# Block 1's first product: three of four pairs by seven products, with operand sums made by adding transfers and on VectorE

## The chip, the cores and the metric

The kernel runs on one core of a Trainium2 chip. The metric is the device time of one execution in microseconds (us); the time of the kernel before is the median of three runs. The engines are TensorE (PE in the profile; its weight loads are PEld), VectorE (DVE), ScalarE (ACT), GpSimd (POOL) and SyncE (SP). SyncE, ScalarE and GpSimd also issue DMA transfers.

## The reference

Inputs: q, k, v of shape (4, 8, 768, 64) (batch, heads, time, head dimension), `w_in` (512, 2048) and `w_out` (2048, 512). First a recurrent attention, then a feed-forward layer with a sigmoid gelu:

```python
for t in range(S):
    state = gamma[None, :, None, None] * state + einsum('bhd,bhe->bhde', k[:, :, t], v[:, :, t])
    y[:, :, t] = scale * einsum('bhd,bhde->bhe', q[:, :, t], state)
x = y.transpose(0, 2, 1, 3).reshape(B * S, H * D)       # 3072 x 512
h = x @ w_in                                            # first product, 3072 x 2048
g = h * (1.0 / (1.0 + exp(-1.702 * h)))
out = g @ w_out                                         # second product, 3072 x 512
```

Everything is float32. The two weights are given as 64-bit floats and are narrowed to float32 in the kernel.

## The kernel before, in words

**Blocks.** The time axis is cut into chunks of 64 steps; one chunk of two batches is 128 tokens, and 24 chunks make 6 blocks of 4 chunks (512 tokens). For each block the attention writes x (for block 1 into `X1`, a view of `W2[:, 6]`), the first product makes the hidden values G, and the second product makes the output. Chunks 0 to 7 (blocks 0 and 1) are attended in an opening part, interleaved with the narrowing of the weights; later chunks are attended between the units of the products.

**Forms of a product.** Blocks 0 and 1 do the first product plainly: `up0` in halves of 256 tokens, `up1` (lines 420 to 428) with all 512 tokens for one of 16 column tiles f of 128 hidden columns. A float32 matmul is two TensorE instructions, so one call of `up1` is 4 matmuls, 8 instructions with 512 moving columns. From block 2 on, `up(d)` (lines 465 to 507) does the first product in the form with seven products in place of eight: a pair d of `w1` pairs (512 hidden columns, 512 tokens) is cut into 2 x 2 quarters, seven products of quarter sums are taken, and the four results are put together by additions. Its operand sums are made ahead on GpSimd (`sums_x`, `sums_w1`). One of its products is 4 matmuls, 8 instructions with 256 moving columns. The second product of blocks 0 and 1 is `down`, also with seven products of 4 units each; later blocks use `down49`.

**Weights.** `W1A` holds the first weight's pairs p = 0 to 3, `W1B` p = 4 to 7; each pair has seven slots of 256 columns, of which slots 0 to 3 are the quarters and slots 4 to 6 hold hidden values of block 0 while that block lasts. The narrowing of one weight tile has the steps `fetch` (a transfer on SyncE, L180), `start` (ScalarE, L207, named `abs` in the written order), `half` (three VectorE instructions, L211 to L213) and `rest` (three, L217 to L222). Three raw buffers take turns, so tile i + 3 is fetched once the `rest` of tile i is done. Tiles 0 to 7 are the first weight, 8 to 15 the second.

**Order.** The opening part is a list of names, written out by hand (lines 845 to 862); each name calls a step of `works`. Steps that go through `pin` keep this order on their engine. TensorE's order is all as written. What isn't pinned (the W2 sums of `sums_w2`, lines 445 to 449, the aging of the state, the loads of later chunks' keys and values) is placed on its engine by the planner of the language. In the opening part `up1.f` is a column tile of block 1's first product and `gate1.f` its gelu on ScalarE (`hidden`, L393), which reads PSUM and writes G. Accumulators in PSUM have two tags, x and y, of two buffers each.

**After the opening part.** The loop over blocks from line 866 on starts with block 0's second product: the units of `P_` in `down`, four (d = 0 to 3) for each of seven products n. Next to unit numbers stand other steps: the W2 sums after units 1, 3, 5 and 7, chunk 8's transposition after unit 2 and its scores after unit 5, chunk 9's transposition after unit 14. `late_loads` (lines 788 to 790) issues the loads of chunks 8 and 9 on SyncE.

Of the kernel before, what the change touches and what calls it, by code (L numbers as in the profile page):

```python
# [13 lines left out]
P = 128  # L14
# [14 lines left out]
def kernel(  # L29
# [38 lines left out]
    CB = 4  # L68
# [43 lines left out]
    def w1(p):  # L112

        return (W1A, p) if p < NP // 2 else (W1B[p // 2 - 2], p % 2)
# [3 lines left out]
    def pin(i):  # L118
        return tc.keep_in_program_order(i) if ordered[0] else i
# [308 lines left out]
        return G[:, p, ab:4:2, :], h  # L428


    def sums_w1(p):
        t, q1 = w1(p)
        w = [t[:, q1:q1 + 2, s] for s in range(7)]
        pool.tensor_add(w[4], w[2], w[3])
        pool.tensor_sub(w[6], w[0], w[2])
        pool.tensor_sub(w[5], w[4], w[0])
        pool.tensor_sub(w[2], w[1], w[5])
# [16 lines left out]
    def sums_g(m, p):  # L454
        a = [g(m, p, s) for s in range(4)]
        tc.keep_in_program_order(dve.tensor_add(a[3], a[2], a[3]))
        tc.keep_in_program_order(dve.tensor_sub(a[2], a[0], a[2]))
        tc.keep_in_program_order(dve.tensor_sub(a[0], a[3], a[0]))

    def sums_g_late(m, p):  # L460
        a = [g(m, p, s) for s in range(2)]
        tc.keep_in_program_order(pool.tensor_sub(a[1], a[1], a[0]))
# [209 lines left out]
    def down(m):  # L672

        acc, kept = {}, {}
        b, t0 = m * CB // NC * 2, m * CB % NC * D
        rows = out.rearrange("(b t) (e c) -> e t b c", b=B, c=EH)[:, t0:t0 + TH, b:b + 2, :] \
            .rearrange("e (h p) b c -> h e p b c", p=P)

        def keep(name, tag, src):
            kept[name] = one.tile([P, 2, EH], F32, name=name, tag=tag)  # L680
            act.activation(kept[name], src, AF.Copy)

        def put(th, e, a, b):
            o = two.tile([P, 2, EH], F32, name="o")
            dve.tensor_add(o, a, b)
            tc.keep_in_program_order((pool if m < NB - 1 else act).dma_start(rows[th, e], o))

        def last_part(d, halves={}):

            n = d // (NP // 4)  # L690
            if d % (NP // 4) == 0:
                halves[n] = ps.tile([P, EH], F32, name="pd", tag="xy"[n])
            for p in range(NP // 2 * (d % 2), NP // 2 * (d % 2 + 1)):
                pe.matmul(halves[n], g1(m, p, 1)[:, n * P:(n + 1) * P], W2[:, 3, p, :], start=(p == 0), stop=(p == NP - 1))
            if d % 2:
                o = two.tile([P, 2, EH], F32, name="o")
                dve.tensor_add(o[:, 0], halves[n], kept["t"][:, n])
                act.dma_start(rows[0, 1][:, n], o[:, 0])

        def part(key, sa, sb, new, last, d, then):  # L700
            if m == NB - 1 and key == "x2":
                last_part(d)
                return
            if d == 0 and new:
                acc[key] = ps.tile([P, 2, EH], F32, name="pd", tag=key[0])
            p0 = acc[key]
            for p in range(2 * d, 2 * d + 2):
                for n in range(2):
                    pe.matmul(p0[:, n, :], g1(m, p, sa)[:, n * P:(n + 1) * P], W2[:, sb, p, :],  # L709
                              start=(new and p == 0 and n == 0), stop=(last and p == NP - 1), skip_group_check=True)  # L710
            if d == NP // 2 - 1:
                then(p0)

        def then_p5(y):
            kept["t"] = one.tile([P, 2, EH], F32, name="t", tag="s1")
            dve.tensor_add(kept["t"], y, kept["u"])

        def then_p7(x):
            keep("vv", "s3", x)
            put(1, 0, acc["y1"], kept["vv"])  # L720
            put(1, 1, acc["y2"], kept["vv"])

        P_ = [("x", 0, 0, True, False, lambda x: keep("p1", "s1", x)),
              ("y0", 1, 2, True, True, lambda y: put(0, 0, y, kept["p1"])),
              ("y1", 3, 1, True, True, lambda y: None),
              ("x", 0, 5, False, False, lambda x: keep("u", "s2", x)),
              ("y2", 3, 4, True, True, then_p5),
              ("x", 2, 6, False, True, then_p7),
              ("x2", 1, 3, True, True, lambda y: put(0, 1, y, kept["t"]))]
        todo = []  # L730
        for n, (key, sa, sb, new, last, then) in enumerate(P_):
            for d in range(NP // 2):
                def unit(key=key, sa=sa, sb=sb, new=new, last=last, d=d, then=then, n=n):
                    part(key, sa, sb, new, last, d, then)
                    if n == 2:
                        sums_g(m, 2 * d)
                    if n == 4 and d == 3:
                        for p in range(0, NP, 2):
                            sums_g_late(m, p)
                todo.append(unit)  # L740
        return todo


# [42 lines left out]
                                        ap=[[0, D], [1, HP]])))  # L786

    def late_loads():
        load(2 * CB, "qkv")
        load(2 * CB + 1, "qk")  # L790

    def halves_anew():

# [15 lines left out]
        "causal": causal, "rows": rows,  # L809
        "rowd": lay_rowd, "whole": lay_whole, "late_loads": late_loads, "anew": halves_anew,  # L810
        "warm": keep_warm}
    for j in range(2 * CB):
        for name in "qkv":
            works[f"{name}{j}"] = lambda j=j, name=name: load(j, name)
        works |= {f"{name}{j}": lambda j=j, do=do: do(j) for name, do in (
            ("turn", turn), ("turned", turned), ("decay", decay), ("masked", masked), ("state", by_state),
            ("x", output), ("aged", aged), ("updated", updated))}
        for f in (None, *range(2 * CB)):
            works[f"step{j}" + ("" if f is None else f"-{f}")] = lambda j=j, f=f: attend(j, f)
        works[f"step-{j}"] = lambda j=j: attend(None, j)  # L820
    for i in range(2 * NFF):
        works[f"w{i // 2}{'ab'[i % 2]}"] = lambda i=i: fetch(i)
    for name, i in [("0a", 0), ("0b", 1)] + [(str(p), 2 * p) for p in range(1, NFF)]:
# [21 lines left out]
    for name in """  # L845
# [8 lines left out]
        half4 gate0.1.5 state5 updated5 anew q6 up0.1.6 x5 rest4 gate0.1.6 abs8 v6 up0.0.6 w7b w7a half8  # L854
        turn6 gate0.0.6 up0.1.0 abs7 half7 gate0.1.0 w9b w9a up0.1.4 q7 gate0.1.4 decay6 step6 masked6 rest7 up0.0.4 v7
        gate0.0.4 turn7 up0.1.3 gate0.1.3 aged6 step7-6 masked7 updated6 decay7 abs9 state6 x6 up0.0.7 rest8 gate0.0.7
        w11a w11b step-7 state7 x7 half9 w10b w10a up0.1.7 rest9 gate0.1.7 abs11 half11 up1.8 gate1.8
        w12a w12b rest11 up1.5 gate1.5 up1.4 gate1.4 abs10 half10 up1.0 gate1.0 rest10 up1.3 gate1.3 abs12
        aged7 updated7 up1.2 gate1.2 w14b w14a half12 up1.6 gate1.6 rest12 up1.9 gate1.9 abs14 half14 w13a w13b
        up1.11 gate1.11 rest14 up1.10 gate1.10 abs13 half13 w15a w15b up1.7 gate1.7 rest13 abs15 half15 up1.12  # L860
        gate1.12 late_loads up1.13 gate1.13 rest15 up1.15 gate1.15 up1.14 gate1.14 up1.1 gate1.1
    """.split():
        works[name]()
    ordered[0] = False
# [92 lines left out]
```

## Time and profile before

| | |
|---|---|
| runs, us | 669.41, 671.01, 666.84; median 669.41 |
| profiled execution, us | 667.55, its span 665.8 |
| TensorE clock granted | 0.995 of full speed |
| TensorE busy | 645.9 us, 97% of the span |
| VectorE busy | 435.1 us, 65% |
| ScalarE busy | 148.2 us, 22% |
| GpSimd busy | 188.7 us, 28% |
| `up1` (L427) in the chain that ended last | 8% of the span |

Times within the profile are counted from the span's start. A busy TensorE is read with care: matmuls overlap, so the cadence of a run of instructions (its length by their number) says more than the duration of one. The chain that ended last is followed back from the last instruction, at each step to what released it. A row of the time line has start, duration, engine, line, operation, output <- input and count; in brackets stands the engine's idle time before it and what ended that.

### The profile page before, as it was taken

The numbers are of one execution on the slowest core, as the hardware profiler recorded it, in microseconds if no ns is written. First come the engines' busy times: TensorE is split into PE (matmuls) and PEld (weight loads), VectorE is DVE, ScalarE is ACT, GpSimd is POOL, SyncE is SP. The second block draws the span as 40 slices with busy tenths as digits, with TensorE's granted clock in tenths as the row PEclk, the third lists the DMA queues.
The fourth block names the chain that finished last, engine by engine and source line by source line (L and its number), as shares of the span: only waits on it lengthen the run. The fifth ranks groups of instructions, "written<-read, shape, count | busy, mean of one in ns | idle before, by whom it ended". The sixth has DMA issues, their size and how long they took to land.

```text
span 665.8 us, 14995 instructions
## 1 busy us (share of the span) xinstructions
PE 645.9 (97%) x6294; PEld 559.1 (84%) x6294; DVE 435.1 (65%) x618; ACT 148.2 (22%) x285; POOL 188.7 (28%) x216
## 2 busy tenths in 40 slices
PE   6789999999999999999999999999999999999997
PEld 3678875446888888888999888999888999988997
DVE  3699878788545775456985354995264995254965
ACT  4674322231000000233100233110233110233110
POOL 6400310000268326100445600354700255500000
PEclk9799999999999999999999999999999999999999
DMA  9996637542203546263385742286652143502142
GB/s 174 205 256 178 186 68 231 166 87 38 43 11 133 172 109 189 56 226 123 89 215 132 230 116 94 75 204 150 189 163 95 62 148 113 222 32 94 49 158 96
DMA packets 146083, 89.48 MB, mean 134 GB/s; under 512 B 131456, under 2 KB 132736, under 8 KB 144992
## 3 DMA queue, kind: packets, MB, share of 16 engines
q1 hardware_dynamic: 135856, 45.19, 30.0%
q0 software_dynamic: 7824, 42.10, 17.8%
q10 hardware_dynamic: 2336, 1.25, 0.6%
q8 instruction: 49, 0.80, 0.5%
q14 instruction: 18, 0.15, 0.1%
HBM read 72.89 MB, written 15.47 MB: 133 GB/s over the span
## 4 chain that ended last, share of the span: by engine, by line
PE 80%; DMA 8%; DVE 4%; SPq 3%; POOL 3%; issue 1%; ACT 0%; DVEq 0%; POOLq 0%; ACTq 0%
PE pq L576 21%; PE px L472 16%; PE pd L709 13%; PE py L472 12%; PE ph L427 8%; PE ph L414 4%; DMA W<-in_moe_w_in_dram 2%; PE pa L289 2%; DMA W<-in_moe_w_out_dram 1%; SPq L157 1%; DMA G<-in_moe_w_in_dram 1%; DMA kn_in<-in_k_dram 1%; PE py L312 1%; PE py L306 1%; DMA k_sq<-in_k_dram 1%
## 5 line engine op out<-in xcount | busy, mean ns | idle before, releaser
L576 PE MATMUL pq<-W,G 128*128 128x128 f32 x672 | 80.5, 276 | 0.7 <-issue 0.7
L545 POOL DMA_DIRECT2D ring<-W2D x28 | 15.4, 552 | 228.9 <-PE px L472 118.2
L576 PEld LDWEIGHTS pq<-W,G 128*128 128x128 f32 x672 | 77.6, 192 | 1.5 <-issue 0.9
L472 PE MATMUL px<-X,W1A 128*128 128x256 f32 x256 | 60.0, 380 | 0.8 <-POOL X L442 0.7
L472 PE MATMUL px<-X,W1B 128*128 128x256 f32 x256 | 59.8, 379 | 0.0
L576 PE MATMUL pq<-ring,own 128*128 128x128 f32 x448 | 59.8, 276 | 0.0
L472 PEld LDWEIGHTS px<-X,W1A 128*128 128x128 f32 x256 | 48.3, 190 | 7.9 <-POOL X L442 1.6
L576 PEld LDWEIGHTS pq<-ring,own 128*128 128x128 f32 x448 | 54.5, 192 | 0.4
L472 PEld LDWEIGHTS px<-X,W1B 128*128 128x128 f32 x256 | 48.6, 190 | 6.7
L709 PE MATMUL pd<-W,G 128*128 128x256 f32 x224 | 49.6, 381 | 0.0
L709 PEld LDWEIGHTS pd<-W,G 128*128 128x128 f32 x224 | 42.2, 190 | 5.8
L472 PE MATMUL py<-X,W1A 128*128 128x256 f32 x192 | 45.4, 379 | 0.0
L472 PE MATMUL py<-X,W1B 128*128 128x256 f32 x192 | 45.4, 379 | 0.0
L393 ACT ACTIVATE G<-G 128x512 f32<-128x512 f32 x48 | 30.2, 630 | 52.0 <-DVE G L482 33.4
L472 PEld LDWEIGHTS py<-X,W1A 128*128 128x128 f32 x192 | 36.5, 190 | 5.0
L472 PEld LDWEIGHTS py<-X,W1B 128*128 128x128 f32 x192 | 36.5, 190 | 4.9
L490 DVE TENSOR_TENSOR t<-py,u 128x512 f32<-128x512 f32 x16 | 11.1, 692 | 33.2 <-PE py L472 33.2
L479 ACT ACTIVATE p<-px 128x512 f32<-128x512 f32 x16 | 9.6, 597 | 94.5 <-PE px L472 94.5
L414 PE MATMUL ph<-X,W1A 128*128 128x256 f32 x128 | 29.0, 382 | 1.4 <-DVE X L347 0.8
L576 PE MATMUL pq<-ring,G 128*128 128x128 f32 x224 | 29.6, 275 | 0.0
L576 PE MATMUL pq<-W,own 128*128 128x128 f32 x224 | 29.6, 275 | 0.0
L504 DVE TENSOR_TENSOR G<-G 128x512 f32<-128x512 f32 (+2 forms) x24 | 12.3, 513 | 25.7 <-ACT G L393 25.7
(207 smaller groups left out, 1168.3 us busy)
## 6 DMA issues: line engine op xcount, KB each, us to landing
ring<-W2D POOLq DMA_DIRECT2D x28, 768.0 KB, 4.7
W1B<-W1D POOLq DMA_DIRECT2D x6, 1792.0 KB, 9.3
W<-in_moe_w_in_dram SPq DMA_DIRECT2D x12, 512.0 KB, 5.3
W<-in_moe_w_out_dram SPq DMA_DIRECT2D x10, 512.0 KB, 5.0
out_dram<-o POOLq DMA_DIRECT2D x20, 256.0 KB, 3.2
q_sq<-in_q_dram SPq DMA_DIRECT2D x144, 32.0 KB, 2.2
k_sq<-in_k_dram SPq DMA_DIRECT2D x144, 32.0 KB, 2.2
v_in<-in_v_dram SPq DMA_DIRECT2D x72, 64.0 KB, 2.7
```

Of the source, the lines that this page charges most:

```text
L157: tc.keep_in_program_order(sp.dma_start(t[r0:r0 + C4, :, n], src[b + r0 // D, :, t0:t0 + C4, r0 % D:r0 % D + C4] .rearrange("h p d -> p h ...
L289: pe.matmul(pa[HALF[w], u, 0, s, :], kt[HALF[u], w, s, :], qt[HALF[u], w, s, :], start=True, stop=True)
L393: pin(act.activation(g, h[:, i], AF.Gelu_apprx_sigmoid))
L414: pe.matmul(h[:, ab], w, X[:, 2 * th + c // 2, c % 2, :], start=(ab == 0 and c == 0), stop=(c == 3), skip_group_check=True)
L427: pe.matmul(h, w, X1[:, c // 2:4:2, c % 2, :], start=(c == 0), stop=(c == 3))
L472: pe.matmul(acc[:, u, :], t[:, q1 + u, sa, c, :], X[:, sb, c, :], start=(start and u == 0 and c == 0), stop=(stop and c == 1), skip_group_ ...
L479: act.activation(p1, x, AF.Copy)
L490: dve.tensor_add(tt, z, u)
L504: dve.tensor_sub(q[0][1], q[0][0], q[0][1])
L545: pool.dma_start(c, W2D[i])
L576: pe.matmul(p0[:, j, :], a[:, d], w[:, d], start=(new and j == 0 and d == 0), stop=(d == NP // 2 - 1), skip_group_check=True)
L709: pe.matmul(p0[:, n, :], g1(m, p, sa)[:, n * P:(n + 1) * P], W2[:, sb, p, :], start=(new and p == 0 and n == 0), stop=(last and p == NP - ...
```

## The change

Of the four pairs of block 1's first product, d = 2 (tiles f = 8 to 11) stays plain and is put in front; d = 0, 1 and 3 are done by seven products (`seven`), in the pattern of `up(d)`.

- The three sums of each pair's weights needed early (w4 = w2 + w3, w6 = w0 - w2, w5 = w4 - w0) are made in `seven_w`: ScalarE copies one operand, with its sign, to a free tile, and a transfer on GpSimd's queue adds the other to it in SBUF. w5 needs w4 landed. The fourth sum (w2' = w1 - w5) is made the same way in `seven_v`, from a negated copy of w5. There are four copies and four transfers of 256 KB for each pair.
- The four sums of x (`seven_x`) are four subtractions on VectorE, once for all pairs.
- In `seven`, products 0, 2 and 4 are copied out of the x accumulator on ScalarE, products 1, 3 and 5 have accumulators of tag y, three results are added on VectorE, and all four go through the gelu.
- The sums lie in tiles that are free at the time: those of q, k, the keys in time order, `tmp`, `qT`, `kT`, `at` and `o`. So chunk 8's and 9's loads move: chunk 8's queries and keys (`qk8`) behind the fetches of tile 15, the rest into `late_loads` at the end.
- The aging and the state update of chunk 7 and the narrowing steps of tiles 10 to 15 are placed anew among the seven products.
- In block 0's second product the first eight units are done in the order n = 0: d 0, 1, 2; n = 1: d 0, 1, 2; n = 0: d 3; n = 1: d 3.

```diff
--- before.py
+++ after.py
@@ -427,6 +427,80 @@
             pe.matmul(h, w, X1[:, c // 2:4:2, c % 2, :], start=(c == 0), stop=(c == 3))
         return G[:, p, ab:4:2, :], h

+
+    SUM_X, SUM_W = {}, {}
+
+    def seven_x():
+
+        for n, (tag, bufs) in ((4, ("q_sq", 2)), (5, ("k_sq", 2)), (6, ("kn", 1)), (2, ("tmp", 1))):
+            SUM_X[n] = two.tile([P, 2, TH], F32, name=f"x{n}", tag=tag, bufs=bufs)
+        for to, a, b in ((SUM_X[4], X1[:, 2], X1[:, 0]), (SUM_X[5], X1[:, 3], SUM_X[4]),
+                         (SUM_X[6], X1[:, 3], X1[:, 2]), (SUM_X[2], X1[:, 1], SUM_X[5])):
+            pin(dve.tensor_sub(to, a, b))
+
+    def seven_w(d):
+
+        t, q1 = w1(2 * d)
+        w = [t[:, q1:q1 + 2, s].rearrange("p u c f -> p u (c f)") for s in range(4)]
+        SUM_W[d] = {4: one.tile([P, 2, 2 * P], F32, name="w4", tag="qT", bufs=2),
+                    5: one.tile([P, 2, 2 * P], F32, name="w5", tag="at", bufs=2),
+                    6: two.tile([P, 2, 2 * P], F32, name="w6", tag="o")}
+        m = SUM_W[d]
+        for to, of, sign in ((4, 2, 1.0), (6, 2, -1.0), (5, 0, -1.0)):
+            pin(act.activation(m[to], w[of], AF.Copy, scale=sign))
+        for to, of in ((m[4], w[3]), (m[6], w[0]), (m[5], m[4])):
+            pin(pool.dma_start(to, of, accum_op=ALU.add))
+
+    def seven_v(d):
+
+        t, q1 = w1(2 * d)
+        m = SUM_W[d]
+        m[2] = one.tile([P, 2, 2 * P], F32, name="w2", tag="kT")
+        pin(act.activation(m[2], m[5], AF.Copy, scale=-1.0))
+        pin(pool.dma_start(m[2], t[:, q1:q1 + 2, 1].rearrange("p u c f -> p u (c f)"), accum_op=ALU.add))
+
+    SEVEN = {}
+
+    def seven(d, k):
+
+        t, q1 = w1(2 * d)
+        a = [G[:, 2 * d:2 * d + 2, s, :] for s in range(4)]
+
+        def product(acc, sa, sb, start, stop):
+            for u in range(2):
+                for c in range(2):
+                    w = SUM_W[d][sa][:, u, c * P:(c + 1) * P] if sa in (4, 5, 6, 2) else t[:, q1 + u, sa, c, :]
+                    x = SUM_X[sb][:, c, :] if sb in SUM_X else X1[:, sb, c, :]
+                    pe.matmul(acc[:, u, :], w, x, start=(start and u == 0 and c == 0), stop=(stop and c == 1),
+                              skip_group_check=True)
+
+        def kept(name, tag, src):
+            SEVEN[name] = one.tile([P, 2, TH], F32, name=name, tag=tag)
+            pin(act.activation(SEVEN[name], src, AF.Copy))
+
+        if k in (0, 1, 3, 5):
+            SEVEN["x" if k == 0 else f"y{k}"] = ps.tile([P, 2, TH], F32, name="ph", tag="x" if k == 0 else "y")
+        acc = SEVEN[f"y{k}" if k in (1, 3, 5) else "x"]
+        product(acc, (0, 1, 5, 4, 6, 2, 3)[k], (0, 1, 5, 4, 6, 3, 2)[k], k in (0, 1, 3, 5), k in (1, 3, 5, 6))
+        if k == 0:
+            kept("p1", "s1", acc)
+        elif k == 1:
+            pin(dve.tensor_add(a[0], acc, SEVEN["p1"]))
+        elif k == 2:
+            kept("u", "s2", acc)
+            hidden(a[0], a[0])
+        elif k == 3:
+            SEVEN["t"] = one.tile([P, 2, TH], F32, name="t", tag="s1")
+            pin(dve.tensor_add(SEVEN["t"], acc, SEVEN["u"]))
+        elif k == 4:
+            kept("vv", "s3", acc)
+        elif k == 5:
+            pin(dve.tensor_add(a[3], SEVEN["y3"], SEVEN["vv"]))
+            pin(dve.tensor_add(a[2], acc, SEVEN["t"]))
+        else:
+            for s in (3, 2):
+                hidden(a[s], a[s])
+            hidden(a[1], acc)

     def sums_w1(p):
         t, q1 = w1(p)
@@ -728,16 +802,19 @@
               ("x", 2, 6, False, True, then_p7),
               ("x2", 1, 3, True, True, lambda y: put(0, 1, y, kept["t"]))]
         todo = []
-        for n, (key, sa, sb, new, last, then) in enumerate(P_):
-            for d in range(NP // 2):
-                def unit(key=key, sa=sa, sb=sb, new=new, last=last, d=d, then=then, n=n):
-                    part(key, sa, sb, new, last, d, then)
-                    if n == 2:
-                        sums_g(m, 2 * d)
-                    if n == 4 and d == 3:
-                        for p in range(0, NP, 2):
-                            sums_g_late(m, p)
-                todo.append(unit)
+        order = [(n, d) for n in range(len(P_)) for d in range(NP // 2)]
+        if m == 0:
+            order[:8] = [(n, d) for ds in ((0, 1, 2), (3,)) for n in range(2) for d in ds]
+        for n, d in order:
+            key, sa, sb, new, last, then = P_[n]
+            def unit(key=key, sa=sa, sb=sb, new=new, last=last, d=d, then=then, n=n):
+                part(key, sa, sb, new, last, d, then)
+                if n == 2:
+                    sums_g(m, 2 * d)
+                if n == 4 and d == 3:
+                    for p in range(0, NP, 2):
+                        sums_g_late(m, p)
+            todo.append(unit)
         return todo


@@ -786,8 +863,8 @@
                                         ap=[[0, D], [1, HP]])))

     def late_loads():
-        load(2 * CB, "qkv")
         load(2 * CB + 1, "qk")
+        load(2 * CB, "v")

     def halves_anew():

@@ -809,6 +886,7 @@
         "causal": causal, "rows": rows,
         "rowd": lay_rowd, "whole": lay_whole, "late_loads": late_loads, "anew": halves_anew,
         "warm": keep_warm}
+    works["qk8"] = lambda: load(2 * CB, "qk")
     for j in range(2 * CB):
         for name in "qkv":
             works[f"{name}{j}"] = lambda j=j, name=name: load(j, name)
@@ -818,6 +896,11 @@
         for f in (None, *range(2 * CB)):
             works[f"step{j}" + ("" if f is None else f"-{f}")] = lambda j=j, f=f: attend(j, f)
         works[f"step-{j}"] = lambda j=j: attend(None, j)
+    works["seven_x"] = seven_x
+    for d in range(NP // 2):
+        works |= {f"seven_w{d}": lambda d=d: seven_w(d), f"seven_v{d}": lambda d=d: seven_v(d)}
+        for n in range(7):
+            works[f"seven{d}.{n}"] = lambda d=d, n=n: seven(d, n)
     for i in range(2 * NFF):
         works[f"w{i // 2}{'ab'[i % 2]}"] = lambda i=i: fetch(i)
     for name, i in [("0a", 0), ("0b", 1)] + [(str(p), 2 * p) for p in range(1, NFF)]:
@@ -854,11 +937,12 @@
         half4 gate0.1.5 state5 updated5 anew q6 up0.1.6 x5 rest4 gate0.1.6 abs8 v6 up0.0.6 w7b w7a half8
         turn6 gate0.0.6 up0.1.0 abs7 half7 gate0.1.0 w9b w9a up0.1.4 q7 gate0.1.4 decay6 step6 masked6 rest7 up0.0.4 v7
         gate0.0.4 turn7 up0.1.3 gate0.1.3 aged6 step7-6 masked7 updated6 decay7 abs9 state6 x6 up0.0.7 rest8 gate0.0.7
-        w11a w11b step-7 state7 x7 half9 w10b w10a up0.1.7 rest9 gate0.1.7 abs11 half11 up1.8 gate1.8
-        w12a w12b rest11 up1.5 gate1.5 up1.4 gate1.4 abs10 half10 up1.0 gate1.0 rest10 up1.3 gate1.3 abs12
-        aged7 updated7 up1.2 gate1.2 w14b w14a half12 up1.6 gate1.6 rest12 up1.9 gate1.9 abs14 half14 w13a w13b
-        up1.11 gate1.11 rest14 up1.10 gate1.10 abs13 half13 w15a w15b up1.7 gate1.7 rest13 abs15 half15 up1.12
-        gate1.12 late_loads up1.13 gate1.13 rest15 up1.15 gate1.15 up1.14 gate1.14 up1.1 gate1.1
+        w11a w11b step-7 state7 x7 seven_w0 half9 w10b w10a up0.1.7 rest9 gate0.1.7 seven_x abs11 half11
+        up1.8 gate1.8 seven_v0 w12a w12b rest11 up1.9 gate1.9 abs10 seven_w1 half10 up1.10 gate1.10 w14b w14a rest10
+        up1.11 abs12 gate1.11 seven0.0 seven0.1 half12 w13a w13b seven0.2 seven0.3 rest12 abs14 seven0.4 seven0.5
+        half14 seven0.6 aged7 seven_v1 w15a w15b qk8 seven1.0 seven1.1 abs13 rest14 seven1.2 seven1.3 updated7 half13
+        seven_w3 seven1.4 seven1.5 abs15 rest13 seven1.6 seven_v3 seven3.0 seven3.1 half15 seven3.2 seven3.3 rest15
+        seven3.4 seven3.5 seven3.6 late_loads
     """.split():
         works[name]()
     ordered[0] = False
```

## The prediction

> **What bounds the kernel now.** I read the chain of work that ended last first, then the stage that is edited, engine by engine, then who makes TensorE wait, then the prices. The chain by line on the page, and in time from 100 to 185 us:
>
> ```profile
> PE 80%; DMA 8%; DVE 4%; SPq 3%; POOL 3%; issue 1%; ACT 0%; DVEq 0%; POOLq 0%; ACTq 0%
> ...
> 100.69 3.65 PE ph L414 x16
> 104.34 54.93 PE ph L427 x128
> 159.27 10.36 PE pd L709 x48
> ```
>
> L427 is block 1's plain first product. Its 128 instructions fill 104.34 to 159.27 without a gap: 54.93/128 = 0.429 us each. (The table's 592 ns for one overlaps its neighbours; only the cadence counts.) What is taken off here comes off the end, if nothing else becomes late. Who makes TensorE wait, over the whole run, longest first:
>
> ```profile
> PE pa L289 <- DVE state L366: 4.1, 1, 4.1
> ...
> PE px L472 <- POOL X L442: 0.7, 1, 0.7
> ```
>
> None of these waits is in this stage and all are small, so a stage that ends earlier should move everything behind it. The stretches of the stage (columns: length; PE, PEld, DVE, ACT, POOL busy with instructions; TensorE clock; DMA share; GB/s):
>
> ```profile
> 104.30:118.00 13.70, 13.70 (x34) 6.05 (x33) 10.96 (x13) 4.50 (x7) 0.00 (x0) 1.00 0.85 272
> 118.00:131.00 13.00, 13.00 (x32) 5.80 (x31) 11.24 (x11) 3.43 (x5) 1.43 (x1) 1.00 0.41 145
> 131.00:145.00 14.00, 14.00 (x34) 6.14 (x33) 10.27 (x11) 5.51 (x7) 0.00 (x0) 1.00 0.59 130
> 145.00:159.30 14.30, 14.30 (x35) 6.41 (x34) 14.06 (x20) 2.39 (x4) 0.00 (x0) 1.00 0.18 29
> ```
>
> TensorE is at full clock, so there is no clock to gain. VectorE is the next busiest by far: it narrows the second product's weights. Its rows:
>
> ```profile
> 104.80 0.70 DVE L217 TENSOR_SCALAR W<-W 128x1024 uint32<-128x1024 uint32 x1
> ...
> 133.51 0.69 DVE L211 TENSOR_SCALAR W<-W 128x1024 f32<-128x1024 f32 x1 [3.65 <-ACT W L207]
> ...
> 150.91 1.23 DVE L222 TENSOR_TENSOR W<-W 128x1024 f32<-128x1024 f32 x1
> 152.17 1.29 DVE L447 TENSOR_TENSOR W<-W 128x512 f32<-128x512 f32 x2
> ```
>
> From 104.80 to the last narrowing step's end at 152.1 it is idle 7.3 us (waits of 1.76, 0.63, 0.34, 3.65 and 0.92) and busy 40.0. ScalarE is busy 4.50 + 3.43 + 5.51 + 2.39 = 15.8 us of 55.
>
> **What the skill says.** "DMA: Bandwidth & Descriptors", "Anatomy of one DMA": a GpSimd transfer takes about 2.0 us plus bytes/436e3. For 256 KB that is 2.6 us; the trace's 256 KB outputs of L686 land after 2.7 us, and its SBUF-to-SBUF pair of 64 KB after 2.3, so it agrees. "Collectives: The Full Stack", "The bandwidth ceiling": an adding transfer costs more than a copy because it needs two source reads, not because of the add. No transfer in this trace adds. "SBUF — State Buffer", "SBUF: two separate sides": VectorE in a two-port mode and GpSimd exclude each other, and GpSimd's descriptor writing stops with it. The trace has one such meeting: L212 at 123.94 us took 1.41 us in place of 0.69 beside GpSimd's L359, which took 1.43 in place of 1.04.
>
> **The change part by part.** *TensorE.* A pair is 32 plain instructions, 32 x 0.429 = 13.73 us. A seven-product pair is 7 x 8 instructions of 256 columns. The same form in later blocks (L472) shows its cadence:
>
> ```profile
> 276.47 3.45 PE px L472 x16
> 279.92 1.73 PE py L472 x8
> ```
>
> 3.45/16 = 0.216 us, so 56 x 0.216 = 12.09. Three pairs save 3 x 1.64 = 4.92 us: the stage would end at 154.35 instead of 159.27. That is the whole credit. The plain pair in front is unchanged work. It ends at 118.07.
>
> *VectorE.* Added: four x sums (4 x 0.69) and three adds per pair (9 x 0.69), with gaps 9.2 us. Nothing is removed. 104.8 + 40.0 + 9.2 = 154.0 even if it never waits, so its 7.3 us of idle time are used up, and it ends level with TensorE. The cover is thin: a delay on VectorE arrives at TensorE through the adds that free accumulators and feed the activations.
>
> *ScalarE.* Sixteen gelu activations stay sixteen (0.60, or 0.63 when read from SBUF). Added: nine copies out of PSUM and twelve weight copies, 21 x 0.6 = 12.6 us, total 28.7 of 50. No bound by amount, but by order: each pair's third product adds into the accumulator that the p1 copy must have read.
>
> *GpSimd queue and transfers.* Twelve adding transfers of 256 KB, issued in some 0.6 us each (L686 0.73, L545 0.55). Per pair: w4 and w6, then w5 after w4 has landed, then w2 after w5 has landed and ScalarE has negated it. GpSimd has only an aging step in this stage; what queues behind its wait is the next transfer. Behind ScalarE's wait for w5 stand the next p1 copy and all that follows. Price of one, issue to landing: 2.3 us is the low end (64 KB, SBUF to SBUF), 5.4 the high end (twice L686: every byte read twice, nothing overlapped). The rows between: ring loads of 768 KB take 4.7, so 704 KB more than 64 cost 2.4, 3.4 ns per KB; 192 KB more than 64 add 0.65, and 256 KB read again 0.87. Estimate: 2.3 + 0.65 + 0.87 = **3.8 us**. A gain isn't possible here: these transfers are new.
>
> *SyncE queue.* Chunk 8's key and value loads, issued from 97.2 us in the trace, partly wait now for the x6 sum's buffer; weight tile 11, which went out at 103.42 behind them, can go when its raw buffer is free (100.5), and arrives some 2.8 us earlier. That removes VectorE's first wait (1.76). Chunk 9's queries and keys wait for the x4 and x5 buffers until about 149 and then take two trains of 4 us. They, and chunk 8's values, are needed only at the 15th unit of block 0's second product and in block 1's: about 180 us and later, covered. Chunk 8's own queries and keys still go out behind weight tile 15, near 131 to 140; needed at the sixth unit, about 165.
>
> *Block 0's second product.* The same 8 units in another order: the fourth group of weights (tile 15) is first needed at the seventh unit, 154.35 + 6 x 1.73 = 164.7, against VectorE's 154.4. No cost. The W2 sums come next on VectorE (7.7 us plus 1.3 of transposes, from 156): done near 165, needed from 168. Cover 3 us; if it fails, TensorE waits by the difference.
>
> **Where the stalls come.** I walked the four queues in the written order with these durations.
> 1. Pair 1's third product is due at 133.4. VectorE reaches pair 0's two last adds only after tile 12's rest, at 130.2 and 130.9. ScalarE then has three gelus, the negated copy for w2 and p1: 130.9 + 3 x 0.63 + 0.62 + 0.6 = 134.0. Stall 0.6.
> 2. Pair 3: its sums start on ScalarE at 137.3, w4's transfer at 137.9; w5 has landed at 137.9 + 2 x 3.8 = 145.5, then negation and p1 until 146.7, due 146.1. Stall 0.6, and 2 us more for each us that a transfer takes longer.
> 3. Twelve transfer issues meet VectorE's two-port steps (some 2.1 us in every 5.85 of a narrowing), at up to 0.7 us each as in the meeting above. Bounds: 0 and 12 x 0.36 x 0.7 = 3 us. I take 1.6, 0.15 on each of the 11 steps of narrowing; of it about 1.1 reaches TensorE (nearly all at pair 1).
>
> Sum: 4.92 saved, 2.2 given back: **2.7 us faster**. Against the profiled execution, 667.55 us (span 665.8 and 1.75 around it), that is 664.9; that execution stands 1.86 under the median of the runs (669.41, from 666.84 to 671.01). On the median: **666.7 us**.
>
> **The rivals.**
> - *Slower: the sums' transfers set the pace.* Place: w5 and w2 of pair 3, and ScalarE standing at the negated copy. For: two transfers in series with only 8 us between the ScalarE slot and the need. Against: 64 KB in 2.3 us and little other traffic after 140. Break-even with the other stalls in place: 3.3 us at pair 3, so a transfer of 5.2 us. At 6 us pair 3 costs 4.8 and the w2 waits begin: about +1.7, 671 us. At 7.5 us pair 0's negated copy stops ScalarE too: stalls 11.8, +6.9, 676.3.
> - *VectorE becomes the bound.* For: 49.2 us of work in 50. If each of its 11 narrowing steps gains 0.3 us, pair 1 waits 2.7 and pair 3 1.1: 3.7 given back, 668.2 us; at 0.5 us (5.7 given back) 670.2. Against: only one stretched step in the trace.
> - *All is hidden.* Transfers at 2.7 us and no lost port time: 0.6 to 0.7 given back, 665.2 us; with no stall at all 664.5.
>
> **How the numbers follow.** The forecast's case 0.48, all hidden 0.15, VectorE 0.17, transfers 0.20 (of which 0.11 beyond 7.5 us). A measurement of this kernel tells some 1% (6.7 us) from no change. The saving cannot exceed 4.9 us, so faster by over 1% is left to scatter alone: 0.04. Slower by over 1% needs transfers beyond 7.5 us, or something unseen: 0.13. The rest, 0.83, is within 1%. Range: 664.5 with 1.5 for scatter below, 663; above, transfers of 6 us (671.1) or VectorE at 0.5 (670.2) with scatter, 673. Both signs lie in it; the likeliest case alone runs from 664.5 to 668.5.
>
> **What would show it.** Right: 32 plain instructions at 0.429 and 168 at 0.216 us; the second product's start near 156.6; TensorE waiting 0.5 to 1.6 us before the third product of pairs 1 and 3, released by ScalarE; transfers landing after 3 to 4.5 us; VectorE without idle time from 108 to 154. Wrong: transfers of over 5 us with ScalarE idle before the negated copies; VectorE's narrowing steps well over 0.69 and 1.23; or a later wait, such as the W2 sums late at 168 or GpSimd's x sums of block 2 late near 264, that eats what the stage gained.

## The result, and the profile after

The changed kernel takes **663.98 us** (median; 660.17 to 669.48) beside 667.48 us for the kernel before in the same comparison (665.12 to 671.01): 0.9946 of the time, with a 95% interval of 0.9926 to 0.9967. That is 3.5 us faster; 2.7 were forecast. Two further comparisons of the same kernel, told below, gave 0.9962 [0.9945, 0.9979] and 0.9968 [0.9951, 0.9985], so 2.1 to 3.6 us by the ratios (1.6 to 3.5 by the medians). The forecast's 666.7 us was counted from a median before of 669.41; counted from 667.48 it is 664.8. The size is right. The profile shows that it isn't made up as forecast.

In what follows the **stage** is block 1's first product, from TensorE's first instruction of it to the first of block 0's second product (`pd`). In the profiled execution of before it runs from 104.17 to 159.11, 54.94 us, by these two rows:

```profile
104.17 3.60 PE L427 MATMUL ph<-W,W1B 128*128 128x512 f32 x8
...
159.11 3.62 PE L709 MATMUL pd<-W,W1A 128*128 128x256 f32 x16
```

In the one of after it runs from 101.13 to 157.01: 55.88 us, **0.9 longer**, though it holds 4.9 us less of TensorE's work. The span is 3.3 us shorter all the same (662.5 to 665.8): the stage began 3.0 us earlier, and what follows it, up to TensorE's last instruction, took 502.0 us where it took 503.1.

The chain of work that ended last, by engine and then in time around the stage, of after. In the part of `seven` it no longer runs through TensorE alone; it passes over w5's transfers of pairs 0 and 3 and the copies on ScalarE:

```profile
PE 77%; DMA 8%; issue 5%; DVE 4%; SPq 2%; POOL 2%; ACT 1%; POOLq 0%; ACTq 0%; DVEq 0%
...
107.56 7.30 DMA w<-w
...
120.58 0.49 ACT p L479
121.11 2.17 PE ph L474 x5
...
143.68 3.34 DMA w<-w
...
148.28 8.90 PE ph L474 x40
```

Who makes TensorE wait, of after. The first line is new, and it is the stage's (L474 is the matmul in `seven`, L479 its copies out of PSUM):

```profile
PE ph L474 <- ACT p L479: 3.7, 2, 2.6
...
PE px L546 <- POOL X L516: 0.8, 1, 0.8
PE pd L783 <- DVE W1B L532: 0.3, 1, 0.3
```

TensorE's time line of after, pair by pair (start, duration, engine, line; in brackets the idle time before and what ended it):

```profile
101.13 13.90 PE L427 MATMUL ph<-W,W1B 128*128 128x512 f32 x32
114.87 3.62 PE L474 MATMUL ph<-W,W1A 128*128 128x256 f32 x16
121.11 7.13 PE L474 MATMUL ph<-x,w 128*128 128x256 f32 x24 [2.63 <-ACT p L479]
128.08 1.89 PE L474 MATMUL ph<-W,w 128*128 128x256 f32 x8
...
131.53 3.62 PE L474 MATMUL ph<-W,W1A 128*128 128x256 f32 x16
...
143.62 3.62 PE L474 MATMUL ph<-W,W1B 128*128 128x256 f32 x16
148.28 5.45 PE L474 MATMUL ph<-x,w 128*128 128x256 f32 x24 [1.04 <-ACT p L479]
...
157.01 3.62 PE L783 MATMUL pd<-W,W1A 128*128 128x256 f32 x16
```

Starts to starts, the plain pair takes 13.74 us, pair 0 16.66, pair 1 12.09 and pair 3 13.39. A pair without a stall is 12.09, so pair 0 gives back 4.57 and pair 3 1.30 us: 5.87 us, more than the 4.92 saved. Pair 0's part has two pieces. Its third product was due at 114.87 + 16 x 0.216 = 118.32 and began at 121.11, 2.79 late. Its 24 instructions then took 6.97 us up to 128.08, 1.78 more than 24 x 0.216. The stretches of after show why in both (columns: length; PE, PEld, DVE, ACT, POOL busy; TensorE clock; DMA share; GB/s):

```profile
101.00:105.00 4.00, 4.00 (x12) 1.82 (x11) 3.90 (x4) 1.32 (x3) 0.00 (x0) 1.00 1.06 282
105.00:110.00 5.00, 5.00 (x13) 2.28 (x12) 4.90 (x8) 1.00 (x2) 0.88 (x1) 1.00 1.15 283
...
121.10:123.00 1.90, 1.89 (x5) 1.54 (x6) 1.87 (x3) 0.00 (x0) 0.61 (x1) 0.52 1.00 148
123.00:125.00 2.00, 2.00 (x7) 1.65 (x6) 1.93 (x4) 0.17 (x1) 0.28 (x1) 0.60 0.61 70
```

After the stall TensorE was granted 0.52 and 0.60 of its clock for four microseconds. And while pair 0's sums were under way, from 101 to 110, the DMA engines were full: share 1.06 and 1.15 (the profile's figure, which can pass 1). The other engines in that time, rows of after's time line (L452 and L460 are the adding transfers as GpSimd issues them, L459 the negated copy of w5, L207 a narrowing's `abs`):

```profile
97.55 2.54 POOL L452 DMA_DIRECT2D w<-W1A  x2 [3.50 <-ACT w L450]
107.56 0.88 POOL L452 DMA_DIRECT2D w<-w  x1 [7.47 <-issue]
114.88 0.63 ACT L459 ACTIVATE w<-w 128x512 f32<-128x512 f32 x1 [8.88 <-DMA w<-w]
117.05 0.69 DVE L211 TENSOR_SCALAR W<-W 128x1024 f32<-128x1024 f32 x1 [3.56 <-ACT W L207]
120.49 0.57 ACT L479 ACTIVATE p<-ph 128x512 f32<-128x512 f32 x1
140.93 2.06 DVE L212 TENSOR_SCALAR W<-W 128x1024 uint32<-128x1024 uint32 x1
```

w4's transfer goes out at 97.55 and lands 9.5 us later; w5's, which needs it, goes out at 107.56, 10.0 us after w4's. (The profile puts GpSimd's wait for it down to "issue", so that it waited for w4 is read from the program and the landing.) w5 lands 7.3 us after that, at 114.86. For the last 8.88 us of that time ScalarE stands at the negated copy, with pair 0's p1 copy, tile 10's `abs` (for which VectorE waits 3.56), pair 1's weight copies and two gelus behind it. Pair 3's sums, in a quieter time, took 4.21 (w4) and 3.34 us (w5).

A full DMA share alone doesn't tell the slow transfers from the quick ones. These are the stretches of after from issue to landing of pair 0's w4, pair 1's w4 and pair 1's w2, in the columns of above:

```profile
97.55:107.03 9.48, 9.48 (x38) 5.81 (x31) 9.08 (x12) 3.04 (x6) 2.54 (x2) 1.00 0.94 261
117.84:121.84 4.00, 1.37 (x5) 0.86 (x5) 3.86 (x5) 3.22 (x6) 2.73 (x2) 0.92 1.00 150
133.61:137.90 4.29, 4.29 (x22) 3.77 (x21) 3.20 (x5) 2.47 (x4) 1.21 (x1) 1.00 1.12 230
```

Pair 0's took more than twice as long at the lower share. Beside it two weight tiles were fetched (SyncE's L180, from 97.33 to 100.26), and one more, from 105.15, just ahead of w5's; between 114.4 and 123.0, with pair 1's w4 in it, none went out. That is no rule either: pair 0's w2, issued 2.3 us after a fetch (113.52), landed after 4.7 us.

### The profile page after: what moved, and what is told of

Same layout as the page of the kernel before. It is cut to its first block, busy times and chain, and to the rows that moved or that the text cites. A ratio compares the mean times of both kernels' runs of the same rounds, so it can differ in the third digit from the quotient of the medians.

```text
span 662.5 us, 15229 instructions
## 1 busy us (share of the span) xinstructions
PE 642.5 (97%) x6366; PEld 573.6 (87%) x6366; DVE 444.8 (67%) x634; ACT 159.1 (24%) x306; POOL 202.6 (31%) x228
## 3 DMA queue, kind: packets, MB, share of 16 engines
q10 hardware_dynamic: 2336, 1.25, 0.6%
## 4 chain that ended last, share of the span: by engine, by line
PE 77%; DMA 8%; issue 5%; DVE 4%; SPq 2%; POOL 2%; ACT 1%; POOLq 0%; ACTq 0%; DVEq 0%
PE pq L650 24%; PE px L546 16%; PE pd L783 13%; PE py L546 12%; PE ph L414 3%; PE ph L474 2%; PE pa L289 2%; DMA w<-w 2%; DMA G<-in_moe_w_in_dram 2%; PE py L312 1%; DMA W<-in_moe_w_out_dram 1%; PE py L306 1%; PE pa L297 1%; SPq L140 1%; DMA k_sq<-in_k_dram 1%
## 5 line engine op out<-in xcount | busy, mean ns | idle before, releaser
L393 ACT ACTIVATE G<-G 128x512 f32<-128x512 f32 x57 | 35.7, 630 | 59.2 <-DVE G L556 33.4
```

The costliest lines, as they stand in the source:

```text
L393: pin(act.activation(g, h[:, i], AF.Gelu_apprx_sigmoid))
```

## The experiments

The theory after the result: the stage's gain is lost at pair 0, because two transfers in series (w4, w5), long because they run among weight fetches and chunk loads, hold ScalarE at the negated copy; the net gain is what is left of 4.92, and something outside the stage. Rivals: the gain comes from the loads on SyncE that the change moved; the adding itself, not the traffic, makes the transfers long; VectorE or the port shared with GpSimd is what holds the stage.

All stages and stalls below are read from the profiled execution of each run in the same way; the times are medians with their ratio to before. "Given back" is the stage less 50.0 us, what it would be without a stall (54.93 - 4.92).

| run | us | ratio to before, 95% | stage, us | given back |
|---|---|---|---|---|
| before again (`e9`) | 667.30 | 0.9997 [0.9982, 1.0011] | 54.93 | - |
| `e4_kn8_late` | 666.66 | 0.9991 [0.9972, 1.0010] | 54.93 | - |
| after | 663.98 | 0.9946 [0.9926, 0.9967] | 55.88 | 5.9 |
| after again (`e1`) | 664.59 | 0.9962 [0.9945, 0.9979] | 54.43 | 4.4 |
| after, third (`e10`) | 666.19 | 0.9968 [0.9951, 0.9985] | 52.85 | 2.8 |
| `e2_v0_late` | 665.79 | 0.9973 [0.9950, 0.9995] | 53.71 | 3.7 |
| `e3_no_transfers` | 662.01 | 0.9912 [0.9880, 0.9945] | 50.10 | 0.1 |
| `e5_sums_early` | 662.54 | 0.9903 [0.9877, 0.9929] | 50.47 | 0.5 |
| `e11_sums_early_again` | 663.19 | 0.9932 [0.9907, 0.9956] | 50.24 | 0.2 |
| `e6_pair0_early` | 663.38 | 0.9919 [0.9887, 0.9950] | 51.06 | 1.1 |
| `e7_plain_copies` | 660.67 | 0.9884 [0.9852, 0.9916] | 50.05 | 0.1 |
| `e8_gpsimd_sums` | 668.76 | 1.0015 [0.9999, 1.0030] | 58.53 | 8.5 |

**The changed kernel again, without an edit.**

> The changed kernel once more, unchanged. In its first profile the stage (first matmul of block 1's first product to first matmul of block 0's second product) took 55.9 us where 50.0 is bare matmul work, and began 3.2 us earlier than in the kernel before (101.1 against 104.3 us). Theory A (the saving is in the stage; stalls differ between executions): the start falls back towards 104 and the stage is shorter than 55, 51 to 54 us. Theory B (the gain comes from the loads of chunk 8 that no longer stand in SyncE's queue before the stage): the start is again near 101 and the stage again near 56. Time by both 662 to 666 us, ratio 0.992 to 0.997.

Stage 54.43, with TensorE waiting 3.02 us before pair 0's third product and 0.77 before pair 3's, both ended by the p1 copy. The stage is shorter and its start, 106.75, lies later than in the first profile; by Theory A it was to fall back towards 104. The stalls stand where the first profile had them, but the clock stayed at 1.00 after the longer wait. So the slow clock is not a fixed part of the price.

**Pair 0's w2 sum later.** The negated copy moves from behind gate1.8 to the end of the plain pair, so ScalarE doesn't stand there.

```diff
-        up1.8 gate1.8 seven_v0 w12a ...
+        up1.8 gate1.8 w12a ...
-        up1.11 abs12 gate1.11 seven0.0 ...
+        up1.11 abs12 gate1.11 seven_v0 seven0.0 ...
```

> The negated copy and transfer for pair 0's fourth weight sum stand behind the last plain gelu in place of the first. Theory A: the wait of ScalarE for w5 of pair 0 (8.9 us) goes, and with it the stall before pair 0's third product (2.8 us and 1.8 us of slow clock after it): 4 to 4.6 us faster than the changed kernel, 659 to 660 us, ratio to before 0.986 to 0.989. Rival (that stall is of the profiled execution only): no more than 1 us faster, 663 to 664 us.

The wait before the third product is gone. In its place the sixth product, which needs w2, waits for w2's transfer. It went out at 120.13, 2.4 us after w5's landing at 117.7, in part because the edit had moved the negated copy back as well, and landed after 8.6 us. TensorE's row of this run:

```profile
128.89 1.97 PE L474 MATMUL ph<-W,w 128*128 128x256 f32 x8 [2.58 <-DMA w<-W1A]
```

The stage is 53.71, inside the spread of the unchanged one, and the time, 665.79 us, missed the forecast of 659 to 660. Freeing ScalarE alone bought nothing that shows: the stall moved down the chain of three transfers.

**No adding transfers.**

```diff
-        for to, of in ((m[4], w[3]), (m[6], w[0]), (m[5], m[4])):
-            pin(pool.dma_start(to, of, accum_op=ALU.add))
...
-        pin(pool.dma_start(m[2], t[:, q1:q1 + 2, 1]..., accum_op=ALU.add))
```

> The twelve adding transfers are left out (the weight sums are then bare copies of one operand, so the values are not the reference's); all copies, adds and products stay. Theory A: the stalls of pairs 0 and 3 go (5.8 us in the profile), the stage takes 50 to 51 us: 658.5 to 660 us. Rival (VectorE's 49 us of work are the bound): the stage still takes over 53 us and the time stays at 662 to 664 us.

Stage 50.10, no wait of TensorE in it, 0.9912. The stage is as forecast; the time, 662.01 us, is above the 658.5 to 660 of Theory A and just in the rival's range, so the stage decides, not the time. All that the stage gives back comes from the transfers, their issue and what waits for them. The copies, adds and x sums that stayed cost TensorE nothing. From TensorE's time line of this run:

```profile
118.93 5.34 PE L471 MATMUL ph<-x,w 128*128 128x256 f32 x24
...
151.84 3.62 PE L780 MATMUL pd<-W,W1A 128*128 128x256 f32 x16
```

**The kernel before, with chunk 8's loads of keys in time order (`kn`) behind its other loads of queries and keys.** This moves those loads alone, none of the rest.

```diff
         def plain(name, src, tag, bufs, engine=sp):
+            keep = tc.keep_in_program_order if j < 2 * CB or j == 2 * CB and name == "kn" else lambda i: i
```

> The kernel before, with chunk 8's key loads pinned behind its queries' on SyncE, so that they no longer go out at 97 us ahead of weight tile 11; nothing else. Theory B (loads out of the way): 2 to 3 us faster than before, 664.5 to 665.5 us. Theory A: within 0.7 us of before, 666.8 to 668.2 us.

Weight tile 11 then goes out at 100.45 us in place of 103.42 (97.33 in after). The ratio is 0.9991, the stage 54.93 and its start 104.16. These loads are not where the gain comes from.

**All sums early.** Each copy and transfer is put well ahead of its use, where its operands have long been ready: pair 0's copies at 79 us, pair 1's at 94.

```diff
-        turn6 gate0.0.6 up0.1.0 ...
+        turn6 gate0.0.6 seven_w0 up0.1.0 ...
-        ... abs9 state6 x6 up0.0.7 rest8 gate0.0.7
+        ... abs9 seven_w1 state6 x6 up0.0.7 rest8 gate0.0.7 seven_v0
-        ... state7 x7 seven_w0 half9 ... gate1.8 seven_v0 w12a ... abs10 seven_w1 half10 ...
+        ... state7 x7 half9 ... gate1.8 w12a ... abs10 half10 ...
-        half14 seven0.6 aged7 seven_v1 w15a w15b qk8 seven1.0 seven1.1 ...
-        seven_w3 seven1.4 seven1.5 abs15 rest13 seven1.6 seven_v3 seven3.0 seven3.1 ...
+        half14 seven0.6 aged7 w15a w15b qk8 seven1.0 seven_v1 seven_w3 seven1.1 ...
+        seven1.4 seven1.5 abs15 rest13 seven1.6 seven3.0 seven_v3 seven3.1 ...
```

> All sums moved away from the fetches of tiles 10 to 14: pair 0's first three into the opening part at about 85 us, its fourth and pair 1's after tile 9's first step at 93 to 100 us, pair 3's beside pair 1's fourth, and pair 3's fourth behind its p1 copy. Theory A (the stalls are the transfers beside saturated DMA engines): no stall over 0.5 us in the stage, which takes 50 to 51 us, as without transfers; time as without transfers, 661 to 663 us, ratio 0.990 to 0.994. Rival (12 issues on GpSimd and their port time cost VectorE as much wherever they stand): the stage takes 52 us or more and the time is that of the changed kernel, 664 us.

Stage 50.47, with no wait over 0.2 us; 0.9903. Nothing is left out here, so this is a usable version that beats the kernel before and, by its ratio, the changed one. TensorE's rows of pair 0's third product and the stage's end:

```profile
121.45 5.34 PE L474 MATMUL ph<-x,w 128*128 128x256 f32 x24
...
154.74 3.62 PE L783 MATMUL pd<-W,W1A 128*128 128x256 f32 x16
```

Pair 0's w4 was little faster here: w5's went out 8.3 us after it, at a DMA share of 1.04 to 1.25; w5 itself landed after 3.6 us. What counts is that the sums had the time: they landed long before their use.

**Pair 0's sums alone early.** Of that edit, `seven_w0` and `seven_v0` only.

```diff
-        turn6 gate0.0.6 up0.1.0 ...
+        turn6 gate0.0.6 seven_w0 up0.1.0 ...
-        w11a w11b step-7 state7 x7 seven_w0 half9 ...
+        seven_v0 w11a w11b step-7 state7 x7 half9 ...
-        up1.8 gate1.8 seven_v0 w12a ...
+        up1.8 gate1.8 w12a ...
```

> Of these moves only that of pair 0's sums. Theory A: the stall before pair 0's third product (4.6 us with the slow clock in the first profile, 3.1 in the second) goes, the one before pair 3's (0.8 to 1.2) stays: stage 51 to 52 us, time 662 to 663.5 us. Rival (as with the late negated copy, another of the transfers then becomes late): stage 53 to 54 us, time about 665 us.

Stage 51.06. The only wait left is pair 3's, 0.80 us. Against the 54.4 that the unchanged kernel's three profiles average, moving pair 0's sums takes 3.3 of the 4.4 us given back. Its w2, put at 101.82 beside the fetches of tiles 10 and 11, took 12.0 us and cost nothing there. That the place makes a transfer long, whichever it is, fits this; no run took the fetches away, so it is argued and not shown.

**Copies in place of adding transfers**, same bytes written, same waits.

```diff
-            pin(pool.dma_start(to, of, accum_op=ALU.add))
+            pin(pool.dma_start(to, of))
```

(and the same in `seven_v`)

> The twelve transfers stay, but copy in place of adding (the sums are then bare operands, so the values are not the reference's). Price of the adding itself: if it costs a second read of every byte, the transfers that have the engines to themselves (pair 1's and 3's last ones, 3.3 to 4.7 us in the changed kernel) land about 1 us earlier, after 2.5 to 3.5 us, and pair 0's first ones, beside the fetches, still take over 7 us. If the adding is the main price, those fall under 5 us too and the stage takes under 52 us. Time 662.5 to 664.5 us.

Stage 50.05 and no wait of TensorE. The issue on GpSimd is shorter, 0.56 us against 0.88 for w5's, as its row in this run shows:

```profile
106.47 0.56 POOL L452 DMA_DIRECT2D w<-w  x1 [4.85 <-issue]
```

It went out 6.3 us after w4's and ScalarE had it 6.9 us later; adding, these were 10.0 and 7.3. So the place and the adding both seem to hold a part, as far as one execution tells: the plain copies of pair 0 too took 5.8 to 6.8 us and two of pair 1 7.9, where the quickest landed in 2.4, and adding put 4 us more on the two of pair 0 (3 to 4.5 against the repeats). Neither branch of the forecast came, and the time, 660.67 us, lies under its 662.5 to 664.5. ScalarE still stood, 3.66 us, but its negated copy began 9.5 us after the stage did. In after it began 13.75, in the repeats 14.1 and 12.55 us after it, and in these three p1 was done 6.2 us later (the work queued between). p1 is needed 13.73 + 3.45 = 17.2 us into the stage, so 11.0 is the limit: 9.5 costs nothing, and the others should make TensorE late by 2.75, 3.1 and 1.55. Pair 0's third product was in fact 2.79, 3.2 and 1.6 late.

**The sums by GpSimd itself**, without copies and transfers.

```diff
-        for to, of, sign in ((4, 2, 1.0), (6, 2, -1.0), (5, 0, -1.0)):
-            pin(act.activation(m[to], w[of], AF.Copy, scale=sign))
-        for to, of in ((m[4], w[3]), (m[6], w[0]), (m[5], m[4])):
-            pin(pool.dma_start(to, of, accum_op=ALU.add))
+        pin(pool.tensor_add(m[4], w[2], w[3]))
+        pin(pool.tensor_sub(m[6], w[0], w[2]))
+        pin(pool.tensor_sub(m[5], m[4], w[0]))
...
-        pin(act.activation(m[2], m[5], AF.Copy, scale=-1.0))
-        pin(pool.dma_start(m[2], t[:, q1:q1 + 2, 1]..., accum_op=ALU.add))
+        pin(pool.tensor_sub(m[2], t[:, q1:q1 + 2, 1]..., m[5]))
```

> The weight sums computed by GpSimd itself (12 tensor operations of 128 x 512) in place of ScalarE's copies and the transfers. If the transfers' latency is what costs, this ends it: sums of a pair in some 5 us without any DMA, stage 50.5 to 52 us, 662 to 663.5 us. If VectorE and GpSimd shut each other out (1.41 for 0.69 and 1.43 for 1.04 us at their meeting in the kernel before), the 12 operations take 1.3 to 2 us each and VectorE loses 6 to 10 us, which TensorE then waits for: stage 54 to 58 us, 665 to 669 us.

It has no transfer to wait for and yet the longest stage, 58.53; 1.0015. A row of TensorE:

```profile
136.64 3.75 PE L472 MATMUL ph<-W,W1A 128*128 128x256 f32 x8 [3.44 <-DVE G L496]
```

Now it is VectorE's adds that come late. GpSimd's operations took 1.26 to 2.25 us, where its operation just ahead, of the same size, took 1.04, and they run beside VectorE's narrowing, whose step L218 took 2.18 us at 131.51 for 1.23 elsewhere. Of the 8.5 us given back, 2.8 are a slow clock after the wait shown: 32 instructions took 9.75 us for 6.9. This is the forecast's VectorE rival, brought about by another edit; in the changed kernel itself it didn't happen.

**Both kernels once more, and the early sums beside them**, to see how much of the difference lies in one execution.

> The kernel before once more. In two profiled executions of its stage (this kernel and the one with the late key loads) it took 54.9 us, and what follows the stage 503.1 and 503.6 us; in the eight profiled kernels with seven products what follows took 501.5 to 503.7, 502.1 on average. If that 1.2 us belongs to the change, what follows takes 503 us or more here too; if it is scatter, it falls to about 502. Stage 54.9 us; time 666 to 669 us.

> The changed kernel a third time. Theory A: the stall before pair 0's third product again, 2 to 3.1 us, released by ScalarE's p1 copy behind the negated copy; stage 53.5 to 56 us; what follows 501.5 to 502.5 us. Time 663 to 666 us.

> The version with all sums moved, again, beside the changed kernel and the kernel before on the same chip. Stage 50.2 to 51 us, no stall over 0.5; 1.5 to 4 us faster than the changed kernel: 660.5 to 663 us, ratio 0.988 to 0.993.

> The kernel before a third time, for its profile. Stage 54.9 us; what follows 503 us or more if that difference belongs to the change, about 502 us if it is scatter.

Before again: 667.30, 0.9997; the stage is 54.93 or 54.94 in all four profiles of kernels without `seven` (before, `e4`, `e9`, `e12`, whose one time was 668.26). The changed kernel's third profile has the stage at 52.85, waits of 1.42 and 0.79, full clock: less than the 53.5 to 56 and the 2 to 3.1 forecast. TensorE's rows of it:

```profile
122.61 5.45 PE L474 MATMUL ph<-x,w 128*128 128x256 f32 x24 [1.42 <-ACT p L479]
...
147.95 5.45 PE L474 MATMUL ph<-x,w 128*128 128x256 f32 x24 [0.79 <-ACT p L479]
```

So the changed stage varies between executions by 3 us, with pair 0's transfers, where the plain one didn't vary in four. The early sums repeated at 0.9932, stage 50.24: 3.0 us under the changed kernel of the same comparison by the medians (663.19 to 666.19), 2.4 by the ratios, with intervals that overlap a little.

**What lies behind the stage.** The changed kernel's three profiles average 54.4 us for the stage, 0.5 saved. The start of the stage averages 103.9 (101.13, 106.75, 103.84) beside 104.2 in the four plain profiles (103.90 to 104.67); it scatters, and of the 3.0 us that it gave the first profile 0.3 is left on the mean. Those 3.0 us stand in the trace long before the first step that the change touches, at the first matmuls of the opening part's first product, before and then after:

```profile
28.27 3.72 PE L414 MATMUL ph<-X,W1A 128*128 128x256 f32 x16 [0.81 <-DVE X L347]
```

```profile
25.11 3.72 PE L414 MATMUL ph<-X,W1A 128*128 128x256 f32 x16 [0.81 <-DVE X L347]
```

(28.44 and 27.41 in the repeats of after), so the change didn't make them. But what follows the stage takes 502.0, 501.5 and 501.3 us after, and 503.1, 503.6, 502.75 and 504.15 in the plain profiles: 1.8 us less. (Of the two that were forecast to take 503 or more if the difference belongs to the change, one did and one fell just short.) From the stage's end to the middle of block 2's second product all seven agree to 0.01 us (175.13 to 175.14). Then the unit up to the next attention step takes 9.13 us in all three of after and 10.07 to 10.62 in all four plain ones, by a pause of TensorE for which the profile knows no cause, each time at the same instruction. TensorE of before, with the pause, up to the attention step:

```profile
337.02 0.39 PE L576 MATMUL pq<-W,G 128*128 128x128 f32 x2
338.08 2.72 PE L576 MATMUL pq<-W,G 128*128 128x128 f32 x22 [0.67 <-issue]
```

and the same 24 instructions of after:

```profile
334.93 2.84 PE L650 MATMUL pq<-W,G 128*128 128x128 f32 x24
```

On the mean of the profiles that unit is 1.2 of the 1.8 us. Up to 0.35 more lies in the stretch with block 3's first product (358.38 to 422.44 in before: 64.06; the plain ones 63.72 to 64.08, after's three 63.73 each), the rest in smaller pieces. I have not tested what causes the pause. Versions of the changed kernel have such pauses too, in other places (`e5` one of 0.60 us, `e6` three of 0.34 to 0.70), so the changed kernel isn't free of them by its nature; its three profiles show none. In the ten profiled kernels with `seven`, what follows the stage took 501.3 to 503.65 us, so the 1.8 us are not certain to belong to the change. Stage, start and remainder give 0.5 + 0.3 + 1.8 = 2.6 us, where the three timed comparisons have 2.1 to 3.6 by their ratios.

## Why the prediction was right, and where it was not

The time was right by luck; two errors of opposite sign met: the stage gave back 4.4 us on the mean of three profiles (3.2 at pair 0, 1.1 at pair 3), not 2.2, and some 1.8 us came from behind it, which no step had.

1. **TensorE's saving, 4.92 us.** Right. Pair 1 took 12.09 us, and without transfers the stage is 50.10.
2. **VectorE, +9.2 us, level with TensorE.** The work was right. It did stand idle, 5.3 us between 102 and 156 in after, mostly for ScalarE's late `abs`, and its narrowing ended at 155.92, 1.1 ahead of the second product. It never made TensorE wait in the stage. The early-sums version has all this work in 50.5 us.
3. **ScalarE by order, not amount.** Right in kind: in all three profiles every stall in the stage was ended by the p1 copy before a third product.
4. **The price of a transfer, 3.8 us.** This is the step that failed, as one price for all twelve. For pair 3 it was right: 4.2 and 3.3 us, 8.1 from w4's issue to w5's landing for the forecast's 7.6. Pair 0's took 9.5 and 7.3, 17.3 from issue to landing. The stretch 104 to 118 us stood in the prediction with a share of 0.85 and 272 GB/s, and none of it went into the price. Why they took so long is not settled: fetches ran beside them, but no run isolates that, and the share alone doesn't explain it. How the price is made up isn't shown either. At w5 of pair 3 a copy took 2.4 for 3.3, and the 0.9 between is what the forecast took for a second read (0.87), but at w2 of pair 3 the copy took 4.3 for 3.8. The 2.6 us estimated for 256 KB from the formula of the Trainium skill ("DMA: Bandwidth & Descriptors", "Anatomy of one DMA") is near the quickest copies (2.4 to 2.8). The issue was priced low too: 0.88 to 1.96 us on GpSimd for 0.6.
5. **Stalls.** Pair 1, 0.6 us forecast: none; its p1 copy ended by 134.1 for a product due at 134.99. Pair 3, 0.6 forecast: its third product was 0.9 to 1.2 late, from w5's landing, as said. Port meetings, 1.1: one row stretched, L212 at 140.93 with 2.06 for 0.69 us, beside GpSimd's aging step (2.04), and no stall came of it. What cost most, pair 0, had none in the forecast. The second product's start, forecast near 156.6, was 157.01, but from an opening 3 us early; in the repeats it was 161.18 and 156.69.
6. **The transfers' rival** had that place: pair 0's negated copy stops ScalarE "at 7.5 us". With 17.3 for the two it was passed, at pair 0 alone; the forecast took 7.5 us as reached by all transfers or by none, with pair 3 the first to fail. That made the rival's total, 676, far too high and the middle way invisible.
7. **Covers.** The reordered units cost nothing. The W2 sums were done at 167.9, 10.9 us after the second product began (10.7 forecast), and nothing waited for them. Tile 11's fetch went out 3.8 us ahead of the stage (97.33), where before it was 0.75 (103.42): 3.05 earlier, 2.8 forecast, and VectorE's first wait (1.76) was gone.

## What to carry to other kernels

A transfer's price belongs to the moment at which it runs: before taking a quiet row's duration, look at what else the DMA engines move in that very stretch and what is issued just ahead, not at their share alone, and add up transfers in series. An in-order engine that waits for a transfer passes the delay to all that is queued behind it; work out when the last of that must be done, and put the chain where that leaves slack, which here brought 2.4 to 3.0 us without removing anything. And where a gain of half a per cent is explained from one profile, profile both kernels again first: the first pair of profiles put it at the start of the stage, where almost nothing of it was.

## What the runs showed of the hardware

- After a wait of 2.63 us TensorE's clock was granted at 0.52 to 0.60 for four microseconds in one execution (1.8 us lost), and at 0.50 after one of 3.44 us in `e8` (eight instructions in 3.54 us for 1.73); after 3.02 us in `e1`, 2.58 in `e2` and 1.42 in `e10` it stayed at 1.00. The length of the wait alone doesn't decide it. The Trainium skill ("TensorE: Matmul & The Clock Gate", "HAM oscillation — how this bites in real kernels") bids to keep such gaps under about 3.4 us; the wait of 2.63 us was shorter and the clock fell after it, so the trace doesn't agree: that bound did not protect here.
- An adding transfer of 256 KB landed after 3.3 to 12.0 us in these runs. The DMA share alone doesn't tell which: 9.5 us at 0.94, 4.0 at 1.00 and 4.3 at 1.12, all in after.
- An adding transfer holds GpSimd longer in its issue than a copy of the same shape: 0.88 against 0.56 us between tiles of sums, 1.2 against 0.70 for w2.
- A pause of TensorE of 0.7 to 1.2 us without a visible cause came at the same place, two matmul instructions into a group of 24, in all four profiles of kernels without `seven`. Its cause is open.
